# Loading V by head group, fewer zero blocks, and a load that waits for a ring buffer

## Chip, core and metric

The kernel runs on one core of one Trainium2 chip. The metric is the device time of one execution in microseconds (us), as the median of several runs. The core has a matrix engine (TensorE, PE in the profile, with its weight loads as PEld), a vector engine (VectorE, DVE), a scalar engine (ScalarE, ACT), a general engine (GpSimd, POOL), a queue engine (SyncE, SP) and 16 DMA engines that move data between the main memory and the on-chip memory.

## What is computed

Softmax attention over 8 batches with 12 heads of 448 tokens and 64 elements, followed by a two-layer network with a SiLU between the layers:

```python
scores = scale * np.matmul(q, k.transpose(0, 1, 3, 2))      # q, k, v: (8, 12, 448, 64)
attn = softmax(scores)
x = np.matmul(attn, v)                                      # then (3584, 768), heads side by side
h = x @ w_in                                                # (768, 2048)
out = (h * 1 / (1 + np.exp(-h))) @ w_out                    # (2048, 768), float32
```

## The kernel before

The 12 heads of a batch are worked in three head groups of four heads. A unit `n` is one head group of one batch: units 0, 1 and 2 are the first batch's, units 3, 4 and 5 the second's, and so on. For each unit the kernel loads the raw keys (`load_k`, line 330) and the raw queries (`load_q`, line 338), each 224 KB as stored on the chip, and VectorE turns them by transposes (`turn_k`, lines 407 and 412, writes the tile `KT`; `turn_q`, line 424, turns the tile `rq` in place). TensorE makes scores `s` from both (`score`, line 460), ScalarE takes their exponentials (lines 505 and 516, tiles `T` and `E`), and TensorE multiplies these with columns of ones for the sums and with V for the result `a` (`attend_alone`, line 568, for the first units; lines 582 and 615 later). VectorE transposes and inverts the sums (lines 640, 648 and 655, tile `rdn`) and scales `a` into `xT` (`norm`, line 685, or 674 for half units). The two products of the network run at line 697, as filler between the attention of later units in the beginning and alone in the end.

All loads go out on POOL's queue in one order, written out by hand near line 1215: keys and queries of unit 0 (its queries in two parts), of unit 1, then the keys of unit 2, the first batch's V in four loads, the queries of unit 2, the keys and queries of unit 3, six loads of `w_in`, and so on. V of a batch is a tile of 128 rows in which a load `x` (0 to 3) fills 32 rows; loads 0 and 1 of the first batch bring four tokens for each row and head, loads 2 and 3 three. In the first batch one load brings this for all twelve heads (192 KB or 144 KB); in later batches each head group has four loads of its own (64 or 48 KB). A rearrangement for unit 1 (`lift_v`, line 372) copies rows of V on VectorE once loads 0 and 1 are there, between the transposition and the inversion of unit 0's sums.

POOL has at most eight loads in flight: each load waits for the landing of the one eight places before it. Tiles come from rings of buffers: raw keys have two (`NRK`), raw queries four, V two. A load into a ring waits until the former tile of its buffer has been read. The raw keys of unit 2 are a special case in this kernel (`GUEST`): they go into a tile `room` that is carved from V's second buffer, which holds nothing until the second batch.

The order of all instructions on every engine is made when the program is built. A planner (class `Order`) runs a small clock with a cost for each operation, keeps a list of those that are ready, and writes the instructions down in the order of its clock; the chip then follows that order, and waits by semaphores. Before the first scores, and where the planner finds TensorE without work in the opening, it fills in products of zeros (`run_zeros`, line 2329), counted in blocks of 128 columns. `FIRST` is the number of blocks in the first such stretch.

```python
    COLD, FIRST, QUIET = 8.5, 47, 0.16
    ...
            if at is not None and len(self.sent) >= LOADS:
                at = max(at, self.sent[-LOADS].done + HOP)
```

Of the kernel before, what the change touches and what calls it, by code (L numbers as in the profile page):

```python
# [9 lines left out]
FP16 = mybir.dt.float16  # L10
# [204 lines left out]
def kernel(  # L215
# [11 lines left out]
    B, NH, S, D = q.shape  # L227
# [3 lines left out]
    NG = NH // HG  # L231
    TPP = S // 32
    NCH = 4
# [6 lines left out]
    NT = 2 * S // 128  # L240
    OH = DM // 2
    NRK, NRQ = 2, 4
    GUEST = (0, 2)
    PACE = 2.6
    BF0 = 4
    NPL = 4
    EAGER = 1
    HALVES = 0
    NEAR, LATE = 0.15, -0.3
    COLD, FIRST, QUIET = 8.5, 47, 0.16  # L250
    SHY = 0.5
    AWAIT = 1.0
    FAR = (NT * B // 4 - 1,)
# [27 lines left out]
    sb = ctx.enter_context(tc.tile_pool(name="sb", bufs=1))  # L281
# [40 lines left out]
    def group_of(src, b, hg):  # L322
        return src[b, HG * hg : HG * (hg + 1)].rearrange("h (i g) d -> (h i) (g d)", g=TPP)

    def load_k(b, hg):
        if (b, hg) == GUEST:
            t = guest
        else:
            t = sb.tile([128, TPP * D], FP16, name=f"rk_{b}_{hg}", tag="rk", bufs=NRK)
        nc.gpsimd.dma_start(out=t, in_=group_of(k, b, hg))  # L330
        rawk[(b, hg)] = t

# [7 lines left out]
    def form(b, hg):  # L340
        return "low" if b == 0 else ("low", "high")[(NG * b + hg) % 2]


    room = sb.tile([128, NH, NCH, D], FP16, name="room", tag="V", bufs=2)
    guest = room.rearrange("p h c d -> p (h c d)")[:, 0 : TPP * D]

    def first_v():
        VT[0] = sb.tile([128, NH, NCH, D], FP16, name="V_0", tag="V", bufs=2)
# [2 lines left out]
    def load_v(b, hg0, hg1, x):  # L351
        if b not in VT:
            VT[b] = sb.tile([128, NH, NCH, D], FP16, name=f"V_{b}", tag="V", bufs=2)
        hs = slice(HG * hg0, HG * hg1)
        kind = form(b, hg0)
        if x == 0 and b > 0 and NG * b + hg0 < ALONE:
            lo = 64 if kind == "low" else 0
            nc.gpsimd.memset(VT[b][lo : lo + 64, hs, place(b, hg0, NCH - 1), :], 0.0)
        first, count = X_TOK[kind][x]
        at = int(kind == "high" and count < NCH)  # L360
        nc.gpsimd.dma_start(  # L361
            out=VT[b][32 * x : 32 * (x + 1), hs, at : at + count, :],
            in_=v[b, hs].rearrange("h (i g) d -> i h g d", g=TPP)[
                :, :, first : first + count, :
            ],
        )
# [25 lines left out]
    def turn_k(b, hg, c0=0, c1=NCH):  # L392
        t = rawk[(b, hg)][:].bitcast(FP32).rearrange("p (g i) -> p g i", i=32)
        if c0 == 0:
            kt = sb.tile([128, TPP, 32, 2], FP16, name=f"KT_{b}_{hg}", tag="KT", bufs=3)
            KT[(b, hg)] = kt
        kt = KT[(b, hg)]
        pairs = kt.rearrange("p g i e -> p (g i e)").bitcast(FP32)
        pairs = pairs.rearrange("p (g i) -> p g i", g=TPP)
        high = form(b, hg) == "high"  # L400
        full = pairs[:, 2 * high : 2 * high + 12].rearrange("p (c x) i -> p x c i", x=4)
        for x in (0, 2):
            first, count = X_TOK[form(b, hg)][x]
            toks = t[:, first : first + 2 * count].rearrange("p (x c) i -> p x c i", c=count)
            at = int(high and count == 4)
            c2 = min(c1, NCH - 1)
            nc.vector.transpose(
                out=full[:, x : x + 2, c0:c2], in_=toks[:, :, at + c0 : at + c2]
            )
            if count == 4 and c1 == NCH:  # L410
                lone = 12 * (not high)
                nc.vector.transpose(out=pairs[:, lone : lone + 2], in_=toks[:, :, 3 - 3 * at])

    def turn_q(n, g0, g1):
        t = rawq[n][:].bitcast(FP32).rearrange("p (g i) -> p g i", i=32)[:, g0:g1]
        if units[n][0] == B - 1:

            to = sb.tile([128, TPP * D], FP16, name=f"q_{n}", tag="rq", bufs=NRQ)
            nc.vector.transpose(
                out=to[:].bitcast(FP32).rearrange("p (i g) -> p g i", g=TPP), in_=t  # L420
            )
            rawq[n] = to
        else:
            nc.vector.transpose(out=t, in_=t)  # L424
        QT[n] = rawq[n].rearrange("p (q e) -> p e q", e=2)
# [29 lines left out]
    def place(b, hg, c):  # L455
        return (c + 1) % NCH if form(b, hg) == "high" else c
# [714 lines left out]
    od = Order(SHY)  # L1171
    s_ring, m_ring, e_ring = Ring(3), Banks((0, 1)), Banks(range(NE))
    rk_ring, rq_ring, v_ring = Ring(NRK), Ring(NRQ), Ring(2)
    kt_ring, t_ring = Ring(3), Ring(NT_)
    ld_k, ld_q, ld_v, ld_win, ld_wout, wout_rows = {}, {}, {}, {}, [], []
    kt_op, qt_op, exp_op, rdn_op, x_op, g_op = {}, {}, {}, {}, {}, {}

    def plan_k(b, hg):
        ring = None if (b, hg) == GUEST else rk_ring
        ld_k[(b, hg)] = od.load(128, 2 * D * TPP, lambda: load_k(b, hg), ring)  # L1180

    def plan_q(n):
        ld_q[n] = [
# [6 lines left out]
            for g0, g1 in (PIECES if n == 0 else ((0, TPP),))  # L1190
        ]

    def plan_v(b, hg0, hg1):
        made = []
        for x in range(4):
            ring = v_ring if (x == 0 and hg0 == 0) else None
            heads, toks = HG * (hg1 - hg0), X_TOK[form(b, hg0)][x][1]
            made.append(
                od.load(32 * heads, 2 * D * toks, lambda x=x: load_v(b, hg0, hg1, x), ring)
            )  # L1200
        for hg in range(hg0, hg1):
            ld_v[(b, hg)] = made
# [9 lines left out]
    def plan_w_out(f0, f1):  # L1212
        wout_rows.append(f0)
        ld_wout.append(od.load(128 * (f1 - f0), 2 * DM, lambda: load_w_out(f0, f1)))

    plan_k(0, 0)
    plan_q(0)
    plan_k(0, 1)
    plan_q(1)
    plan_k(0, 2)  # L1220
    plan_v(0, 0, NG)
    plan_q(2)
    plan_k(1, 0)
# [7 lines left out]
    plan_q(5)  # L1231
    plan_w_out(0, 4)
    plan_v(1, 0, 1)
    plan_w_out(4, 8)
    plan_w_out(8, 12)
    plan_v(1, 1, 2)
    plan_w_out(12, 16)
    plan_v(1, 2, 3)
    for n in range(NB0 + NG, NU):
        b, hg = units[n][:2]  # L1240
# [6 lines left out]
    def plan_turns(upto):  # L1247

        while turned["n"] < min(upto, NU):
            if not plan_turn(turned["n"]):  # L1250
                return
            turned["n"] += 1

    def plan_turn(n):
        b, hg, g0, g1 = units[n]
        if b == B - 1 and not rq_ring.can(1, od.now):
            return False
        if (b, hg) not in kt_op:
            if not kt_ring.can(1, od.now):
                return False  # L1260
            kt_ring.take()
            first = Op(
                "DVE", 0.73, lambda: turn_k(b, hg), [ld_k[(b, hg)]], 20,
                then=None if (b, hg) == GUEST else rk_ring.give,
            )
            if n == 0:
                first = Op("DVE", 0.4, lambda: turn_k(b, hg, 0, 2), [ld_k[(b, hg)]], 20)
            kt_op[(b, hg)] = od.add(first)
        if b == B - 1:
            rq_ring.take()  # L1270
        qt_op[n] = [
            od.add(
                Op(
                    "DVE",
                    0.13 + (g1 - g0) / 30.0,
                    lambda g0=g0, g1=g1: turn_q(n, g0, g1),
                    [load],
                    20,
                    then=rq_ring.give if b == B - 1 else None,
                )  # L1280
            )
            for load, (g0, g1) in zip(ld_q[n], PIECES if n == 0 else ((0, TPP),))
        ]
        if n == 0:
            rest_k.append(
                od.add(
                    Op(
                        "DVE",
                        0.45,
                        lambda: turn_k(b, hg, 2, NCH),  # L1290
                        [kt_op[(b, hg)], qt_op[0][0]],
                        20,
                        then=rk_ring.give,
                    )
                )
            )
        return True
# [1129 lines left out]
```

## Time and profile before

| what | value |
|---|---|
| median of 3 runs | 377.55 us (377.43 to 378.58) |
| the profiled execution's own time | 377.82 us |
| its span, first to last instruction | 376.0 us |
| PE busy | 370.4 us, 98% of the span |
| DVE busy | 292.4 us, 78% |
| ACT busy | 255.6 us, 68% |
| POOL busy | 85.0 us, 23% |
| loads of the first 45 us, POOL's queue | 8.29 MB |
| DMA rate from 5 to 7 us, and from 13 to 15 us | 122 and 209 GB/s |

How to read it: lines such as `L361` are lines of the kernel. The page has the busy time by engine and by 40 slices of the span, and the chain of work that ended last, followed back from the end: what share of it lay on which engine. A timeline line gives the start in us, the time that it took, engine, line, operation, the tile written and read, and how many instructions are merged; in square brackets stands how long the engine was idle before it and what released it. A line of DMA issues gives the tiles, the queue, how many were issued, the size of one, and the time from its issue to its landing in us. A landing time of a single load below is its issue plus that time.

### The profile page before, as it was taken

To read this page: it belongs to the slowest core of one execution; us is meant where nothing else is said; L and a number is where in the kernel's file an instruction comes from. 1 tells how busy PE (TensorE), PEld (TensorE's weight loads), DVE (VectorE), ACT (ScalarE), POOL (GpSimd) and SP (SyncE) were. 2 spreads that over 40 slices of the span, in tenths; PEclk is the share of its full clock that TensorE was granted. 3 is DMA by queue.
4 is the path that set the end of the run, shared out by engine and by line. 5 is a ranking of instruction groups with operands and counts; after the bars stand their busy time and mean duration, and the time that the engine had idled before them with its cause. 6 is when DMAs were issued, how large, how long until landed. Compare 5 with 4: busy or idle time off the path is not lost.

```text
span 376.0 us, 10031 instructions
## 1 busy us (share of the span) xinstructions
PE 370.4 (98%) x4052; PEld 189.3 (50%) x4052; DVE 292.4 (78%) x613; ACT 255.6 (68%) x402; POOL 85.0 (23%) x155
## 2 busy tenths in 40 slices
PE   8999999999999999999999999999999999999996
PEld 3365445444444444444444444545556765556774
DVE  3667958999995969995969998899579744648883
ACT  4988873887878788777878777658872238883121
POOL 7552437424016326006423200000000000000000
PEclk9999999999999999999999999999999999999999
DMA  7999999919049948147964421210001241000144
GB/s 112 198 208 210 206 204 183 199 18 135 14 99 137 171 51 120 30 94 106 171 97 57 60 53 45 53 34 0 0 3 46 63 107 39 0 3 26 50 115 150
DMA packets 35967, 34.49 MB, mean 92 GB/s; under 512 B 11856, under 2 KB 35152, under 8 KB 35920
## 3 DMA queue, kind: packets, MB, share of 16 engines
q0 software_dynamic: 25312, 22.82, 41.1%
q1 hardware_dynamic: 10064, 10.40, 10.2%
q8 instruction: 32, 0.52, 0.6%
q10 hardware_dynamic: 544, 0.62, 0.5%
q14 instruction: 15, 0.12, 0.1%
HBM read 45.61 MB, written 11.01 MB: 151 GB/s over the span
## 4 chain that ended last, share of the span: by engine, by line
PE 97%; DMA 1%; issue 0%; POOL 0%; DVE 0%; POOLq 0%
PE p L697 28%; PE h L697 21%; PE f L697 16%; PE s L460 12%; PE a L582 8%; PE o L697 3%; PE a L568 2%; PE n_Q L697 2%; PE a L615 2%; PE n_P L697 2%; DMA rq<-in_q_dram 1%; PE z L2329 1%; PE z L697 0%; PE z L568 0%; DVE ost L1033 0%
## 5 line engine op out<-in xcount | busy, mean ns | idle before, releaser
L516 ACT ACTIVATE E<-s 128x896 f16<-128x896 f32 x164 | 142.0, 919 | 24.8 <-PE s L460 24.7
L697 PE MATMUL h<-xT,w_in_t 128*32 128x448 f16 (+2 forms) x762 | 83.5, 348 | 0.0
L697 PEld LDWEIGHTS <-w_in_t 128*128 128x128 f16 (+1 forms) x909 | 54.6, 97 | 50.0 <-issue 8.1
L361 POOL DMA_DIRECT2D V<-in_v_dram x88 | 48.5, 565 | 49.7 <-PE a L582 29.2
L697 PEld LDWEIGHTS <-G 128*128 128x128 f16 (+1 forms) x652 | 40.1, 97 | 26.0 <-issue 5.0
L729 ACT ACTIVATE th<-h 128x448 f16<-128x448 f32 x67 | 36.6, 546 | 24.3 <-PE h L697 20.7
L697 PE MATMUL p<-w_out_t,G 128*128 128x384 f16 (+1 forms) x294 | 46.7, 327 | 0.0
L460 PE MATMUL s<-rq,KT 32*128 32x448 f16 (+3 forms) x728 | 44.9, 347 | 0.5 <-DVE rq L424 0.5
L697 PEld LDWEIGHTS <-S 128*128 128x128 f16 (+1 forms) x329 | 29.9, 98 | 21.3 <-issue 3.4
L773 DVE SCALAR_TENSOR_TENSOR G<-th,h 128x448 f16<-128x448 f16 (+1 forms) x64 | 35.7, 573 | 4.7 <-ACT th L729 4.3
L697 PE MATMUL p<-D,S 128*128 128x384 f16 (+1 forms) x217 | 39.3, 327 | 0.0
L1027 ACT COPY ost<-p 128x384 f32<-128x384 f32 x36 | 17.3, 480 | 26.8 <-PE p L697 24.2
L582 PE MATMUL a<-E,V 128*32 128x448 f16 (+1 forms) x640 | 32.7, 356 | 0.0
L685 DVE SCALAR_TENSOR_TENSOR xT<-a,rdn 128x448 f16<-128x448 f32 x46 | 26.9, 618 | 3.4 <-PE a L582 2.2
L338 POOL DMA_DIRECT2D rq<-in_q_dram x25 | 13.9, 558 | 67.0 <-PE s L460 58.2
L460 PEld LDWEIGHTS <-KT 32*128 32x128 f16 (+1 forms) x824 | 12.4, 96 | 31.0 <-issue 29.2
L529 DVE TENSOR_TENSOR T<-T,E 128x1792 f16<-128x1792 f16 x21 | 22.8, 1086 | 4.8 <-ACT E L516 4.8
L529 DVE TENSOR_TENSOR T<-E,E 128x1792 f16<-128x1792 f16 x21 | 22.7, 1082 | 4.1 <-ACT E L516 4.0
L901 DVE TENSOR_TENSOR p<-f,p 128x448 f32<-128x448 f32 x15 | 9.3, 623 | 20.3 <-PE f L697 13.9
L1049 DVE TENSOR_TENSOR ost<-p,ost 128x384 f32<-128x384 f32 x28 | 15.4, 552 | 12.2 <-ACT ost L1027 7.7
L697 PE MATMUL f<-sx,tw 128*128 128x448 f16 x102 | 23.7, 353 | 0.0
L582 PEld LDWEIGHTS <-V 128*32 128x32 f16 (+1 forms) x640 | 13.5, 95 | 18.0 <-issue 10.1
(140 smaller groups left out, 483.9 us busy)
## 6 DMA issues: line engine op xcount, KB each, us to landing
out_dram<-ost SPq DMA_DIRECT2D x146, 48.0 KB, 2.2
rk<-in_k_dram POOLq DMA_DIRECT2D x23, 224.0 KB, 5.3
rq<-in_q_dram POOLq DMA_DIRECT2D x23, 224.0 KB, 5.9
w_out_t<-in_moe_w_out_dram POOLq DMA_DIRECT2D x4, 768.0 KB, 12.6
V<-in_v_dram POOLq DMA_DIRECT2D x42, 64.0 KB, 4.4
out_dram<-wide SPq DMA_DIRECT2D x48, 48.0 KB, 1.6
V<-in_v_dram POOLq DMA_DIRECT2D x42, 48.0 KB, 4.6
w_in_t<-in_moe_w_in_dram POOLq DMA_DIRECT2D x6, 256.0 KB, 9.2
```

Source lines behind the costliest of these rows:

```text
L338: nc.gpsimd.dma_start(out=rawq[n][:, cols], in_=group_of(q, b, hg)[:, cols])
L361: nc.gpsimd.dma_start(out=VT[b][32 * x : 32 * (x + 1), hs, at : at + count, :], in_=v[b, hs].rearrange("h (i g) d -> i h g d", g=TPP)[:, : ...
L460: nc.tensor.matmul(out=pS[p0 : p0 + 32 * (x1 - x0), h % 2, at : at + q1 - q0], lhsT=KT[(b, hg)][32 * h : 32 * (h + 1), key_rows(b, hg, c, ...
L516: nc.scalar.activation(out=E[(n, w)][:, 2 * y : 2 * y + 2, :], in_=pS_t[(n, w, y)][:, :, 0:S], func=AF.Exp, scale=attn_scale,)
L529: nc.vector.tensor_tensor(out=T[n], in0=T[n] if step else E[(n, 0)], in1=E[(n, step + 1)], op=ALU.add,)
L582: nc.tensor.matmul(out=a[32 * h : 32 * (h + 1), 0:S], lhsT=VT[b][k0:k1, HG * hg + h, place(b, hg, c), part - 1 :: 2], rhs=e[k0:k1, h], sta ...
L685: nc.vector.scalar_tensor_tensor(out=x3(b, cc)[:, cc % 3, 32 * g0 : 32 * g1], in0=acc[(n, part)][:, 0:nq], scalar=0.5, in1=rdn_t[n].rearra ...
L697: nc.tensor.matmul(out=out[i : i + cut], lhsT=w[:, i : i + cut], rhs=x, start=start, stop=stop, skip_group_check=True,)
L729: nc.scalar.activation(out=th, in_=h_t[(b, f, t0)][:, 0:n], func=AF.Tanh)
L773: nc.vector.scalar_tensor_tensor(out=dst[:, f, at + lo : at + hi], in0=th_t[(b, f, t0)][:, lo - t0 : hi - t0], scalar=1.0, in1=h_t[(b, f, ...
L1027: nc.scalar.copy(out=ost(qd, *OUT[m]), in_=bank(qd, BANK[m]))
L1049: nc.vector.tensor_tensor(out=t, in0=bank(qd, BANK[m]), in1=t, op=ALU.add)
```

## The change

Three things are changed. The first batch's V is loaded in eight loads: the four of the first head group (64, 64, 48 and 48 KB), then the four of the other two groups together (128, 128, 96 and 96 KB). The planner's own count stays at four loads; the last of them emits five. The first stretch of zeros has 44 blocks for 47, and the later stretches of the opening, which the planner sizes itself, come out as 9, 7, 9 and 13 blocks where they had 8, 11, 9 and 13. And the raw keys of unit 2 take a buffer of the ring of raw keys like all others, so their load waits until VectorE has turned the keys of unit 0; the tile `room` is gone. Apart from this every engine has the same instructions in the same order as before.

```diff
-    GUEST = (0, 2)
-    COLD, FIRST, QUIET = 8.5, 47, 0.16
+    COLD, FIRST, QUIET = 8.5, 44, 0.16
...
     def load_k(b, hg):
-        if (b, hg) == GUEST:
-            t = guest
-        else:
-            t = sb.tile([128, TPP * D], FP16, name=f"rk_{b}_{hg}", tag="rk", bufs=NRK)
+        t = sb.tile([128, TPP * D], FP16, name=f"rk_{b}_{hg}", tag="rk", bufs=NRK)
...
-    room = sb.tile([128, NH, NCH, D], FP16, name="room", tag="V", bufs=2)
-    guest = room.rearrange("p h c d -> p (h c d)")[:, 0 : TPP * D]
...
     def plan_k(b, hg):
-        ring = None if (b, hg) == GUEST else rk_ring
-        ld_k[(b, hg)] = od.load(128, 2 * D * TPP, lambda: load_k(b, hg), ring)
+        ld_k[(b, hg)] = od.load(128, 2 * D * TPP, lambda: load_k(b, hg), rk_ring)
...
+    def in_turn(b, hg0, hg1, x):
+        if b:
+            return load_v(b, hg0, hg1, x)
+        load_v(0, 0, 1, x)
+        if x == 3:
+            for y in range(4):
+                load_v(0, 1, NG, y)
+
     def plan_v(b, hg0, hg1):
...
-                od.load(32 * heads, 2 * D * toks, lambda x=x: load_v(b, hg0, hg1, x), ring)
+                od.load(32 * heads, 2 * D * toks, lambda x=x: in_turn(b, hg0, hg1, x), ring)
...
-                then=None if (b, hg) == GUEST else rk_ring.give,
+                then=rk_ring.give
```

More of the change, by code (lines that the diff above doesn't have):

```diff
@@ L1262, in plan_turn @@
             first = Op(
-                "DVE", 0.73, lambda: turn_k(b, hg), [ld_k[(b, hg)]], 20,
-                then=None if (b, hg) == GUEST else rk_ring.give,
+                "DVE", 0.73, lambda: turn_k(b, hg), [ld_k[(b, hg)]], 20, then=rk_ring.give
             )
```

## The prediction

> **What bounds the kernel now.** I read the page's head and its chain of waits first, then the chain for the first 45 us, then POOL's and DVE's timelines there, then single DMA issues with their time to landing. Of the page:
>
> ```profile
> span 376.0 us, 10031 instructions
> DMA  7999999919049948147964421210001241000144
> PE 97%; DMA 1%; issue 0%; POOL 0%; DVE 0%; POOLq 0%
> ```
>
> TensorE sets the end (97% of the chain). From 24 us on it never pauses, so what the opening loses or wins reaches the end one for one, and the change touches only the opening. There the DMA engines are full (the row of nines). The chain of waits from 0 to 45 us:
>
> ```profile
> 2.48 4.71 DMA rq<-in_q_dram
> ...
> 13.93 0.75 PE s L460 x8
> 14.68 0.57 issue
> 15.25 0.94 PE a L568 x16
> ...
> 19.90 0.65 PE s L460 x24
> 20.55 0.87 PE a L568 x16
> ```
>
> The 0.57 us before 15.25 are a wait for the first batch's V (the weights of that first `a` are V). After it TensorE runs on. What POOL issues meanwhile, and DVE's part where groups 2 and 3 arrive:
>
> ```profile
> 4.04 0.58 POOL L330 DMA_DIRECT2D room<-in_k_dram  x1
> 4.55 2.52 POOL L361 DMA_DIRECT2D V<-in_v_dram  x4
> 7.47 0.57 POOL L338 DMA_DIRECT2D rq<-in_q_dram  x1 [0.40 <-DMA rq<-in_q_dram]
> 9.40 0.55 POOL L330 DMA_DIRECT2D rk<-in_k_dram  x1 [1.36 <-DVE KT L412]
> 10.22 0.53 POOL L338 DMA_DIRECT2D rq<-in_q_dram  x1 [0.28 <-DMA rq<-in_q_dram]
> ...
> 6.01 0.20 DVE L407 STREAM_TRANSPOSE KT<-rk 128x64 f32<-128x64 f32 x1
> 18.89 0.65 DVE L424 STREAM_TRANSPOSE rq<-rq 128x448 f32<-128x448 f32 x1
> 19.46 0.61 DVE L640 STREAM_TRANSPOSE rdn<-a 128x448 f32<-128x448 f32 x1
> ```
>
> POOL starts each load only when the one eight places earlier has landed: its ninth and later loads follow a landing by 0.3 us (0.55 with a second wait). DVE turns the fourth q (group 0 of batch 1) at 18.89, as soon as it has landed.
>
> ```profile
> rq<-in_q_dram POOLq DMA_DIRECT2D x1, 224.0 KB, 8.3
> ...
> rk<-in_k_dram POOLq DMA_DIRECT2D x1, 224.0 KB, 8.8
> ...
> rq<-in_q_dram POOLq DMA_DIRECT2D x1, 224.0 KB, 8.6
> ...
> rq<-in_q_dram POOLq DMA_DIRECT2D x1, 224.0 KB, 4.0
> ```
>
> These are issues at 7.47, 9.40, 10.22 and 102.87 us: the first three stand 8 to 9 us in a full queue; the last one, alone, needs 4.0.
>
> **The change part by part.** The profiled execution took 377.82 us (span 376.0, 1.8 around it); the median of the runs is 377.55, so differences are worked out in the trace and added to 377.55.
>
> *Zero blocks, 47 to 44.* The first stretch (12 products, 1.00 to 6.04, 0.107 us a block) ends 0.32 earlier. The first score needs q turned at 5.42+0.41=5.83, and starts 0.05 after such a turn (7.62 to 7.67), so at 5.88 for 6.04: at most 0.16 won. Later stretches lose three more blocks in sum (9, 7, 9, 13 for 8, 11, 9, 13) under ACT's cover: ACT runs from 6.66 to 16.48 without a pause. ACT's third exponential needs the second score (7.67 to 8.25), which doesn't move, so no more than 0.1 passes on. I take 0, bounds -0.16 and, should the clock rise late, +0.9 (below).
>
> *V of head group 0 first.* Its four loads (64, 64, 48, 48 KB) need not wait for all 672 KB. Keys of group 2 landed at 4.04+7.6=11.7, and the 192 KB V loads behind it landed at 4.55+7.9=12.4 and 1.0 later, so 224 KB more are there by 12.9, well before 14.68. The 0.57 us wait goes. How much is kept: the next score's second half writes a bank that ACT frees at 15.68 and now starts at 16.13, so at most 0.45; with the zero blocks at most 0.55 in all. DVE's copy of V rows (14.66, before the reciprocal) now waits for the first two of the second four loads; issued near 9.2 and 9.8 they land by about 13.9 with the stream: covered by 0.7. The last V load is needed at 18.97 only.
>
> *Group 2's raw keys in the buffer of group 0's.* The load now waits until DVE has turned group 0's keys (6.01+0.20). POOL starts it at about 6.5 instead of 4.04. Queued behind it on POOL stand all eight V loads, then q2, k and q of batch 1, all w_in; SP's queue isn't touched. The landing itself hardly moves: q1, ahead of it in the stream, lands only at 9.95, and one load behind it is 11.1 to 11.7. Its scores come at 17.50, 5 us after its turn.
>
> *Eight loads for four.* POOL spends 4 x 0.54 = 2.2 us more (the pace of V loads at 42.5 to 44.1). Worse, the eight loads in flight now hold fewer bytes (all of V's 672 KB takes eight places, not four). With the eight-back rule: 6.5 (keys), V at 7.05, 7.6, 8.1, 8.7, 9.2, 9.8, 10.4; the last V load must wait for the keys' landing, 11.66+0.28, so 11.9; q2 at 12.5, k(1,0) 13.1, q3 13.6, where it was 7.47, 9.40, 10.22. By then the stream has almost run dry: the last V load lands near 11.9+2.3=14.2 (2.3 is a lone 64 KB load at 111.60). So q2 pays the lone latency: 12.5+4.0=16.5 (15.8 before). The next two follow at 1.25 us (two neighbours at 113.76 and 114.31 landed 3.9 and 4.6 after issue, so 1.25 apart): 17.75 and 19.0. In the window of 10 to 20 us one 16 KB instruction fetch occupies one engine for 0.96 us (0.6% of 16 engines in 10 us); before, k(1,0) landed 2.4 after q2, so I read it as hitting this pair, and add it: q3 at 19.96, before 10.22+8.6=18.85. It is 1.1 us later.
>
> *Who waits for that.* DVE turns q3 at 18.89, then `rdn` at 19.46, which frees the bank of the `a` at 20.48 (0.41 spare); further down the same row of DVE work, `xT` at 21.13 to 22.29 lets `a` start at 22.47, with 0.2 spare, the least. So TensorE is 1.1-0.2=0.9 us later, and what V won at 15 us is waited away at 20. Later loads shift by the same 1.1 or less, and TensorE by then stands 0.9 later itself.
>
> Bounds of that term: with no idle queue and no fetch on the path, q3 lands as before and TensorE keeps up to -0.45; with 4.6 for the lone load (issue at 181.03), 1.25 twice and a fetch that costs all of k's excess (2.4-1.15=1.25), q3 is at 20.85, +2.0, so +1.8. I take 0.9: the spacing rows are two neighbours with the same sizes. Sum: 0 - 0.57 + 0.57 (waited again) + 0.9 = +0.9, so 377.55+0.9=**378.45 us**; the profiled execution would be 378.7.
>
> By the Trainium skill, *DMA: Bandwidth & Descriptors*, "Rules for kernel authors", transfers of 64 KB and less are mostly overhead and should be joined. Rows here: V loads issued at 42.50 (64 KB) and 43.04 land 9.2 and 8.9 us later, so 0.24 us apart, which bytes alone explain. By the rule with a fixed 2 us for each of the four added loads in series, an estimate from that page, the time would be some 8 us more, 385.5; the rows deny it while the queue is full, and it gets no chance.
>
> **The rivals.**
> *A, not slower:* the stream never runs dry. For it: keys 1 and q1 land late (8.8, 9.95) and V's bytes go on behind them, so q2 may still find a queue, and loads behind a queue land 1.1 apart. It decides at a landing of q3 of 19.05, 0.2 late: with it on time -0.2 is left of V's gain, 0.25 sooner -0.45; about 377.2. Against it: q2's issue moves by 5 us.
> *B, more than that:* early loads land faster because POOL writes no descriptors from 4.1 to 6.5 (the DMA rate is only 122 GB/s from 5 to 7 us, 205 later). Even then ACT's unbroken row caps the gain at 0.55: 377.0.
> *C, dry sooner:* the keys, issued at 6.5, land as slowly as keys 1 did (issued 3.00, landed 8.83: 5.8 us), at 12.3. The last V load and all behind it start 0.65 later, q3 1.75 late: 377.55+1.55=379.1.
> *D, the clock:* the pause before the first score (5.71 to 5.88) keeps the clock low longer. A block took 0.107 us up to 6.04 and 0.064 in the stretch at 8.25, so the rise came about 6. Staying low to 9 would double the scores at 6.04 (+0.5) and 8.89 (+0.9), and ACT would be up to 0.9 late: partly under the late q3, so 378.9. The Trainium skill, *TensorE: Matmul & The Clock Gate*, Part 1, has the clock judged over free-running windows of 3.4 us; by that rule a 0.17 us pause in one is nothing, and an unlucky phase hits both kernels alike. No row tells which.
>
> **How the numbers follow.** Forecast (q3 0.5 to 1.9 late): 0.58; A 0.16; B 0.05; C 0.14; D 0.07. 0.3% is 1.13 us, about what a measurement here can tell from no change: below 376.42 or above 378.68. The forecast's own range, 377.85 to 379.4, lies half beyond 378.68 as the fetch falls (0.29); with C and half of D that makes slower 0.46; the other half of the forecast, A, half of D and the rest make same 0.50; faster gets 0.04 out of B's share, for a cap that I misread, since nothing found reaches -1.13. Range 377.0 to 379.9: from B's cap to C with a fetch's excess (+0.8) on top.
>
> **What would show it.** In the profile after: no idle time before the first `a` with V, near 14.7; POOL's keys of group 2 near 6.5, q2 near 12.5, q3 near 13.6; DVE's turn of q3 near 20 with idle time before it that names the DMA; TensorE idle near 20 to 21 us; all of it unchanged from 45 us on but for the shift. Wrong if q3's turn stays at 18.9 (A), if the keys land after 12 (C), or if the zero blocks at 8 us still take 0.107 each (D).

## The result, and the profile after

| | before | after |
|---|---|---|
| median, runs of the same session | 377.47 us (377.23 to 378.58, 8 runs) | 379.23 us (378.71 to 381.08, 8 runs) |
| ratio after to before | | 1.0053, 95% interval 1.0038 to 1.0069 |
| the profiled execution's own time | 377.82 us | 379.20 us |
| its span | 376.0 us | 377.3 us |

The changed kernel is 0.53% slower, 1.8 us by the medians, and more than the 0.3% that can be told from no change. The two profiled executions stand 1.38 us apart, since the one of before lies 0.35 above its median.

The head of the page after, and its chain of work that ended last:

```profile
span 377.3 us, 10038 instructions
...
PE 88%; DMA 8%; POOL 1%; DVE 1%; issue 1%; POOLq 0%
```

TensorE held 97% of this chain before. Now 88% of it is left, and DMA has 8%: loads have come onto the path. The chain from 0 to 45 us shows which ones (start, duration, what):

```profile
6.51 4.48 DMA rk<-in_k_dram
...
11.28 0.49 POOL V L354
...
16.26 10.26 DMA w_in_t<-in_moe_w_in_dram
...
27.07 13.57 DMA rq<-in_q_dram
...
40.66 0.65 DVE rq L417
...
41.86 1.30 PE h L690 x6
```

These lines go from the load of unit 2's keys through the last V load, which waits for those keys' landing, and through a `w_in` load to the queries of unit 5, which land at 27.07 + 13.57 = 40.6 us. VectorE turns them, and a product of the network starts late behind it. POOL in the opening:

```profile
6.51 0.53 POOL L326 DMA_DIRECT2D rk<-in_k_dram  x1 [2.44 <-DVE KT L400]
7.03 3.92 POOL L354 DMA_DIRECT2D V<-in_v_dram  x7
11.28 0.58 POOL L354 DMA_DIRECT2D V<-in_v_dram  x1 [0.32 <-DMA rk<-in_k_dram]
11.85 0.57 POOL L334 DMA_DIRECT2D rq<-in_q_dram  x1
```

POOL stands idle for 2.44 us before the keys. Then it issues without a pause until 17 us, but for the 0.32 before the last V load. The queries of unit 2 (`q2`) start at 11.85; before it was 7.47. What TensorE and VectorE make of it, with the first scores of unit 2 before the change as the line ahead:

```profile
17.50 0.77 PE L460 MATMUL s<-rq,KT 32*128 32x224 f16 x16
```

```profile
14.45 0.56 PE L561 MATMUL a<-T,V 128*32 128x448 f16 x8
...
18.59 0.58 PE L453 MATMUL s<-rq,KT 32*128 32x224 f16 x16 [1.59 <-DVE rq L417]
...
41.86 1.30 PE L690 MATMUL h<-xT,w_in_t 128*128 128x448 f16 x6 [0.30 <-DVE G L766]
```

```profile
17.89 0.65 DVE L417 STREAM_TRANSPOSE rq<-rq 128x448 f32<-128x448 f32 x1 [1.31 <-DMA rq<-in_q_dram]
20.01 0.65 DVE L417 STREAM_TRANSPOSE rq<-rq 128x448 f32<-128x448 f32 x1 [0.29 <-DMA rq<-in_q_dram]
```

The first product with V starts at 14.45 and no longer waits (15.25 before). That lead of 0.8 is lost at 18.59, where TensorE waits 1.59 us for `q2` (this score stood at 17.50 before), and from 19 us on each product starts 0.9 later than before. At 41.86 this becomes 1.37 (the same product stood at 40.49), and it stays so.

One reason why `q2` is late is the DMA rate. Below are three stretches of 2 us, before and then after. The columns are: busy time and number of instructions on PE, PEld, DVE, ACT and POOL, granted clock, mean load of the DMA engines, GB/s.

```profile
11.00:13.00 2.00, 2.00 (x31) 0.55 (x19) 0.76 (x3) 2.00 (x3) 1.00 (x2) 1.00 1.51 192
13.00:15.00 2.00, 1.68 (x26) 0.53 (x24) 0.96 (x3) 2.00 (x4) 1.62 (x3) 1.00 1.32 209
15.00:17.00 2.00, 1.75 (x32) 0.74 (x36) 1.59 (x5) 1.75 (x3) 1.59 (x3) 1.00 1.13 207
```

```profile
11.00:13.00 2.00, 2.00 (x28) 0.64 (x20) 0.76 (x3) 2.00 (x4) 1.72 (x4) 1.00 1.15 135
13.00:15.00 2.00, 2.00 (x36) 0.76 (x32) 0.95 (x3) 2.00 (x4) 2.00 (x4) 1.00 1.18 152
15.00:17.00 2.00, 2.00 (x35) 0.54 (x24) 1.47 (x4) 2.00 (x4) 1.95 (x3) 1.00 1.13 151
```

The stream of loads runs at 135 to 152 GB/s where it ran at 192 to 209. At 11.0 us before had 1,568 KB issued and not landed (keys of unit 2, all of V, `q2`, keys and queries of unit 3). After, where the keys had just landed, had 576 KB: seven V loads, none of them over 128 KB. By 13.0 us it is 1,120 KB against 1,664 KB.

A second reason is likely: one late part. A load ends in 16 parts. Of `q2`'s, fifteen were there by 16.89 us and the last at 17.87. A 16 KB instruction fetch stood on a DMA engine from 15.42 to 17.15 us (1.73 us); before, it stood there from 16.07 to 16.96, when `q2` had landed. The trace does not say which engine carried the late part, so that the fetch made up about 1 us of the 2.15 by which `q2` landed late is not shown.

### The profile page after: what moved, and what is told of

Read it like the earlier page. It is cut to its first block, busy times and chain, and to the rows that moved or that the text cites. A ratio compares the mean times of both kernels' runs of the same rounds, so it can differ in the third digit from the quotient of the medians.

```text
span 377.3 us, 10038 instructions
## 1 busy us (share of the span) xinstructions
PE 370.3 (98%) x4051; PEld 189.2 (50%) x4051; DVE 292.2 (77%) x613; ACT 255.6 (68%) x402; POOL 87.0 (23%) x159
## 4 chain that ended last, share of the span: by engine, by line
PE 88%; DMA 8%; POOL 1%; DVE 1%; issue 1%; POOLq 0%
PE p L690 28%; PE h L690 18%; PE f L690 16%; PE s L453 9%; PE a L575 8%; DMA rq<-in_q_dram 5%; PE o L690 3%; DMA w_in_t<-in_moe_w_in_dram 3%; PE n_Q L690 2%; PE a L608 2%; PE n_P L690 2%; DMA rk<-in_k_dram 1%; POOL w_in_t L372 1%; PE a L561 0%; POOL rk L326 0%
## 5 line engine op out<-in xcount | busy, mean ns | idle before, releaser
L354 POOL DMA_DIRECT2D V<-in_v_dram x92 | 50.5, 562 | 51.2 <-PE a L575 29.2
L690 PEld LDWEIGHTS <-S 128*128 128x128 f16 (+1 forms) x329 | 29.9, 98 | 21.2 <-issue 3.4
L453 PEld LDWEIGHTS <-KT 32*128 32x128 f16 (+1 forms) x824 | 12.5, 96 | 33.0 <-issue 29.8
L894 DVE TENSOR_TENSOR p<-f,p 128x448 f32<-128x448 f32 x15 | 9.4, 624 | 20.3 <-PE f L690 13.9
```

Source lines behind the costliest of these rows:

```text
L354: nc.gpsimd.dma_start(out=VT[b][32 * x : 32 * (x + 1), hs, at : at + count, :], in_=v[b, hs].rearrange("h (i g) d -> i h g d", g=TPP)[:, : ...
L453: nc.tensor.matmul(out=pS[p0 : p0 + 32 * (x1 - x0), h % 2, at : at + q1 - q0], lhsT=KT[(b, hg)][32 * h : 32 * (h + 1), key_rows(b, hg, c, ...
L690: nc.tensor.matmul(out=out[i : i + cut], lhsT=w[:, i : i + cut], rhs=x, start=start, stop=stop, skip_group_check=True,)
```

## The experiments

Three names are used below. Theory N: the number of loads is the cost (places in the window of eight, and POOL's 0.55 us for each). Theory P is N at work after a stall: POOL, once late, issues without a pause, and small loads feed the stream too slowly. Theory G: the wait of unit 2's keys is the cost. Ratios are to runs of before on the same chip, with 95% intervals; 0.1% is 0.38 us.

**V in eight loads, alone.** The edit, to the kernel before:

```diff
+    def in_turn(b, hg0, hg1, x):
+        if b:
+            return load_v(b, hg0, hg1, x)
+        load_v(0, 0, 1, x)
+        if x == 3:
+            for y in range(4):
+                load_v(0, 1, NG, y)
```

> The kernel before with the first batch's V in eight loads and nothing else: the third group's keys still go into V's idle buffer, 47 zero blocks. Theory N (number of loads): a load starts only when the one eight places earlier has landed, so with eight small V loads in the eight places q2, k and q of batch 1 start near 12.0 to 13.6 us for 7.5 to 10.2, the stream of loads thins out and q2 lands 1 to 2 us late: +0.9 to +1.8 us against before, most of the change's whole +1.76. Theory G (the keys' wait is what starves the stream, POOL idle from 4.1 to 6.5): without that wait V's first group arrives early and nothing is late: -0.5 to 0.

Measured: 378.53 us for 377.62, ratio 1.0035 (1.0018 to 1.0052). N's time holds, and G falls as the only cause: with the keys' load at 4.03 us and POOL never kept waiting for a buffer, the loss is there. POOL waited 0.4 to 0.9 us before each of the last four V loads for the landing eight places back, and `q2` started at 11.47. By itself this is about two thirds of the change's loss.

N's way to that time does not hold. `q2` landed at 15.47, 0.25 sooner than before, where 1 to 2 us late was expected, and up to 56 us TensorE stands 0.2 ahead of the trace of before. But the `w_in` loads behind are 0.9 late at their median part, and the lag stays. TensorE falls behind at the first product with `w_out` (0.1 at 56.7 us) and at 73 to 76 us (0.5), behind queries that landed at 70.13 for 68.85. POOL's timeline, and VectorE's at those queries:

```profile
8.73 0.58 POOL L361 DMA_DIRECT2D V<-in_v_dram  x1 [0.92 <-DMA rk<-in_k_dram]
...
11.47 0.57 POOL L338 DMA_DIRECT2D rq<-in_q_dram  x1
```

```profile
70.15 0.65 DVE L424 STREAM_TRANSPOSE rq<-rq 128x448 f32<-128x448 f32 x1 [0.47 <-DMA rq<-in_q_dram]
```

**The keys' wait, alone.** The edit, to the kernel before:

```diff
-    GUEST = (0, 2)
...
-        if (b, hg) == GUEST:
-            t = guest
...
-        ring = None if (b, hg) == GUEST else rk_ring
```

> The kernel before with one part of the change: the third group's keys wait for a buffer of raw keys; V in four loads, 47 zero blocks. Theory N: POOL's loads start at 6.5 (keys), 7.1 to 8.9 (V), 9.5 (q2), 10.1 (k), 10.7 (q3), which the full stream still hides: -0.1 to +0.3 us. Theory G: the stream has 224 KB less in flight from 4.6 to 7 us and never gets it back, loads land 1 us or more late: +1.0 to +1.8.

Measured: 377.93 for 377.62, ratio 1.0009 (1.0001 to 1.0018): 0.3 us, at the upper edge of N's range and far below G's. The keys started at 6.59, `q2` at 9.55 and landed 0.36 later than before; from the first `w_in` load to unit 5's queries, landings agree with before within 0.25 us (the median parts are 0.6 to 0.8 late). Here the stall of 2.5 us on POOL, with large loads behind it, is nearly made good.

**44 zero blocks, alone.**

```diff
-    COLD, FIRST, QUIET = 8.5, 47, 0.16
+    COLD, FIRST, QUIET = 8.5, 44, 0.16
```

> The kernel before with 44 zero blocks for 47 and nothing else. Theory: the first score starts 0.15 us earlier (5.9 for 6.04), of which ACT's row passes on 0 to 0.1: -0.15 to +0.05 us. Rival D (the pause before the first score keeps the clock low): +0.5 to +1.0, and the blocks at 8 us take 0.107 each.

Measured: 377.47 for 377.62, ratio 0.9999 (0.9990 to 1.0008). Rival D is out. In the trace the first score came at 6.02, not 5.9, since its queries landed 0.13 later; the pause before it was there.

**V in six loads, keys in the idle buffer, 44 zero blocks.**

```diff
+    SPLIT = (2, 3)
+        if b or x not in SPLIT:
+            return load_v(b, hg0, hg1, x)
+        load_v(0, 0, 1, x)
+        if x == 3:
+            for y in SPLIT:
+                load_v(0, 1, NG, y)
```

> The kernel before with 44 zero blocks and V in six loads: x 0 and x 1 whole, then x 2 and x 3 of head group 0, then x 2 and x 3 of the other two groups; the keys still go into V's idle buffer. Head group 0's V is then complete 192 KB earlier in the stream, some 0.9 us at the 205 GB/s of before. Theory N: the loads behind start at 9 to 12 us, while some 600 KB or more are still queued, so nothing of the stream is lost and the wait of 0.57 before the first product with V goes: -0.55 to -0.3 us. Rival (each added small load costs the stream its own fixed time, some 0.4 us): -0.1 to +0.5, with q2 landing 0.5 to 1 us late.

Measured: 378.24 for 377.62, ratio 1.0011 (1.0001 to 1.0022); the theory's gain is missed. The rival's time came, though `q2` landed 0.4 sooner than before and not later. In the one trace the wait at 15 us is gone, TensorE stands 0.33 ahead of the trace of before, and no `w_in` load lands later. But this execution took 377.48, the fastest of eleven. What the slower ones lost was not traced.

**The changed kernel with the idle buffer given back.** The edit, to the changed kernel:

```diff
+    GUEST = (0, 2)
...
+        ring = None if (b, hg) == GUEST else rk_ring
```

> The changed kernel with one part undone: the third group's keys go into V's idle buffer again; V in eight loads and 44 zero blocks stay. If the parts simply add (V in eight alone measured +0.35%, the keys' wait alone +0.09%, the zero blocks 0), this is +0.8 to +0.9 us against before, and the changed kernel's other 0.9 us come only from both parts together. Theory P (POOL's pace: after its stall from 4.1 to 6.5 it issues without a pause to 13.5, and small loads of 64 and 48 KB every 0.55 us supply less than the stream can carry) says the same, +0.5 to +1.0, with the w_in loads about 0.9 us late instead of 2.5. Rival (the loss is all in the eight loads, and the difference of the first runs is scatter): +1.6 to +1.9.

Measured: 378.92 for 377.66, ratio 1.0031 (1.0019 to 1.0043). So eight loads with the idle buffer lose about 1.2 us, and without it 2.0. The 1.2 lies between P's range (up to 1.0) and the rival's (from 1.6). The wait that costs 0.3 alone costs 0.8 on top of eight loads; that difference between intervals is likely, not certain. The expected 0.9 us for the `w_in` loads held at the first of them and had grown to 1.7 by the sixth. (Such lags of the stream are those of the median of a load's 16 parts; a landing is the last part.)

**V's first four loads ahead of the keys.** The edit, to the changed kernel; the second four stay behind the keys:

```diff
-        load_v(0, 0, 1, x)
-        if x == 3:
-            for y in range(4):
-                load_v(0, 1, NG, y)
+        load_v(0, 1, NG, x)
...
+    def after_v(b, hg):
+        if (b, hg) == (0, 2):
+            for x in range(4):
+                load_v(0, 0, 1, x)
+        load_k(b, hg)
```

> The changed kernel with one place in POOL's queue changed: the four loads of V's first head group go ahead of the third group's keys, so POOL has work from 4.1 to 6.5 us while the keys' buffer is still in use; eight V loads, no idle buffer used, 44 zero blocks. Theory P: POOL's stall is filled, keys start at 6.5 as in the changed kernel, q2 near 11, and the stream is about 0.9 us late at the w_in loads (as with the eight loads alone) for 2.5: +0.3 to +1.0 us against before. Rival G (the keys themselves come too late): they land later still, behind 224 KB of V, near 11.5 to 12, so no better than the changed kernel: +1.6 to +2.0.

Measured: 378.78 for 377.66, ratio 1.0034 (1.0021 to 1.0047): 1.1 to 1.3 us, between P's range and G's and nearer to P's. The keys landed 0.2 later than before and 0.8 later than in the changed kernel, at no cost (at 17.5 us TensorE is 0.5 ahead of before), and the first `w_in` load was 0.7 late for 2.45. The stall was worth about 0.7 us of the loss; the eight loads kept the rest.

**`q2` ahead of the last two V loads.**

```diff
         if x == 3:
-            for y in range(4):
-                load_v(0, 1, NG, y)
+            load_v(0, 1, NG, 0)
+            load_v(0, 1, NG, 1)
+
+    def then_v(n, g0, g1):
+        load_q(n, g0, g1)
+        if n == 2:
+            load_v(0, 1, NG, 2)
+            load_v(0, 1, NG, 3)
```

> The changed kernel with q2 taken ahead of the last two of V's eight loads, nothing else. POOL's stall and the number of loads are those of the changed kernel. Theory P: q2 starts near 10.4 for 11.85 and brings 224 KB into a queue that only held small loads, so it lands near 15.5 to 16.5 for 17.87, the wait of 1.6 us at 17 goes and the w_in loads are 1.5 to 2.2 us late for 2.5: +0.4 to +1.2 us against before. Rival (the stream's rate, not POOL's order, is low while POOL writes descriptors): what q2 gains k and q3 lose, and the w_in loads stay 2.5 late: +1.3 to +2.0.

Measured: 379.40 for 377.66, ratio 1.0053 (1.0039 to 1.0067): nothing won. The rival's time came, and what `q2` gained unit 3's queries lost, as it said. `q2` landed at 16.22 as expected, and the wait only moved on. TensorE's timeline of this kernel:

```profile
17.72 0.58 PE L453 MATMUL s<-rq,KT 32*128 32x224 f16 x16 [0.51 <-DVE rq L417]
...
21.05 0.40 PE L453 MATMUL s<-rq,KT 32*64 32x224 f16 x15 [0.60 <-DVE rq L417]
```

Less is lost at 17.7, and what is saved there is lost again at 21.05, at unit 3's queries, which landed 1.46 late. The `w_in` loads were 1.8 to 2.0 late, within P's bounds and not the rival's 2.5; P's price for that lag was too low.

**V in five loads, keys in the idle buffer, 44 zero blocks.** The edit, to the kernel of six:

```diff
-    SPLIT = (2, 3)
+    SPLIT = (3,)
```

> The kernel before with 44 zero blocks and V in five loads: x 0 to 2 whole, x 3 of head group 0, then x 3 of the other two groups; the keys still go into V's idle buffer. Head group 0's V is then complete 96 KB earlier in the stream, 0.47 us at 205 GB/s. If one added load costs the stream nothing: -0.4 to -0.1 us. If each added load costs what six loads seem to (their median +0.1% in spite of the wait removed): 0 to +0.3.

Measured: 377.63 for 377.66, ratio 0.9999 (0.9991 to 1.0008). One added load costs nothing; the wait at 15 us that it removes brings nothing in the median either.

**Unit 5's keys and queries ahead of three `w_in` loads**, in the changed kernel and, as its control, in the kernel before.

```diff
-    plan_w_in(1024, 2048)
     plan_k(1, 2)
     plan_q(5)
+    plan_w_in(1024, 2048)
```

> The changed kernel with the loads of keys and queries of unit 5 taken ahead of the three w_in loads of 512 KB (they come 7.5 us of stream earlier, those w_in loads 2.2 us later). In the changed kernel's trace unit 5's queries land at 40.63, 2.2 late, and hold DVE and then TensorE at 41.86 (offset +0.91 before, +1.37 behind). Theory S (the lag of the stream of loads lands on TensorE twice, at q2 and at these queries): the wait at 41.86 goes and the offset stays +0.9: +0.8 to +1.4 us against before, 0.4 to 0.9 less than the changed kernel. Rival (the first wait, at q2, sets all, or the lag only finds the next load): +1.6 to +2.1.

> The same move of unit 5's keys and queries on the kernel before: the control for the run before this one. No wait for these queries stands in the trace of before (they land at 38.45 and are turned at once), and the three w_in loads come 2.2 us later but before their first product: -0.3 to +0.3 us against before by theory S and by its rival. More than +0.3 would say that the move itself costs, and has to be taken off the other run.

Measured: 379.99 for 377.60, ratio 1.0067 (1.0053 to 1.0082), and for the control 377.75, ratio 0.9998 (0.9989 to 1.0007). The changed kernel with the move lost 2.5 us, more than either range. Theory S, that the lag bites at `q2` and at these queries and nowhere else, falls. TensorE's timeline in the changed kernel with the move:

```profile
41.81 0.55 PE L690 MATMUL h<-xT,w_in_t 128*128 128x448 f16 x2 [1.42 <-DMA w_in_t<-in_moe_w_in_dram]
```

The same place is now held by a `w_in` load, and for longer (in this execution, the slowest of its six, the stream was over 3 us late, and `q2` had landed 2.8 late before the move could matter). The move itself is free where the stream is on time.

**V in five loads, four of them ahead of the keys; no idle buffer** (the aims of the change with larger loads).

```diff
+        if (b, hg) == (0, 2):
+            for x in range(3):
+                load_v(0, 0, NG, x)
+            load_v(0, 0, 1, 3)
+        load_k(b, hg)
```

> The changed kernel's aims with other loads: V in five loads (x 0 to 2 whole, x 3 of head group 0, x 3 of the rest), the first four of them ahead of the third group's keys, which wait for a buffer of raw keys; no idle buffer used, 44 zero blocks. POOL then has large loads to start from 4.1 to 6.5 us and the window of eight holds as many bytes as before. Theory P and S: w_in loads within 0.3 us of before, V in time for the first product: -0.3 to +0.3 us against before, 1.5 less than the changed kernel. Rival (the keys' wait costs by itself, since they land near 13.5 and their turn holds DVE ahead of the first normalisation at 14): +0.5 to +1.0.

Measured: 378.00 for 377.60, ratio 1.0014 (1.0003 to 1.0024). The 0.4 to 0.5 us lie between P's range and the low end of the rival's. P is right about the stream: no `w_in` load lands later than before, and of the changed kernel's 2.0 us about 1.5 are gone. The rival's mechanism is there too. VectorE's timeline:

```profile
13.80 0.38 DVE L400 STREAM_TRANSPOSE KT<-rk 128x192 f32<-128x192 f32 x1 [3.71 <-DMA rk<-in_k_dram]
```

The keys, now behind 576 KB of V, are turned at 13.80 for 11.68 and push the first normalisation from 13.98 to 14.49.

**Four loads of 256 bytes behind V's four** (read by nobody).

```diff
+    aside = const.tile([32, 4, 4], FP16, name="aside")
...
+        if b == 0 and x == 3:
+            for y in range(4):
+                nc.gpsimd.dma_start(out=aside[:, y, :], in_=v[0, 0][32 * y : 32 * (y + 1), 0:4])
```

> The kernel before with four added loads of 256 bytes each (32 partitions x 4 numbers, never read) behind V's four loads; V, keys' buffer and the 47 zero blocks as before. It moves no bytes to speak of, only takes four places of the eight and four of POOL's 0.55 us. Theory N (places and POOL's time are the cost of the eight loads): q2, k and q of batch 1 start near 12.0 to 12.7, 13.0 to 13.8 and 13.8 to 14.5 us for 7.5, 9.4 and 10.2, loads from w_in on are 0.5 to 1.5 us late, and the time is +0.5 to +1.5 us against before, about that of V in eight loads alone (+1.3 by its ratio). Rival (V's cut rows, 64 and 48 KB over 32 partitions, move more slowly by themselves): with V uncut nothing is lost, -0.1 to +0.3.

Measured: 379.19 for 377.57, ratio 1.0046 (1.0032 to 1.0060). The loss, 1.6 to 1.7 us, is just above N's range, and so is the lag of the `w_in` loads (2.0 to 2.4 at the median part). This decides for N against cut rows of V: V's loads, the keys' buffer and the zeros are those of before, 1 KB is added, and nearly the whole loss of the change is there. Nor is it the added bytes' own transfer: their 128 packets took 2.9 us in sum, 0.2 us of 16 engines. POOL's timeline, and two stretches of 2 us (columns as above):

```profile
6.98 0.59 POOL L1198 DMA_DIRECT2D aside<-in_v_dram  x1
8.30 0.51 POOL L1198 DMA_DIRECT2D aside<-in_v_dram  x1 [0.73 <-DMA rk<-in_k_dram]
9.45 0.49 POOL L1198 DMA_DIRECT2D aside<-in_v_dram  x1 [0.65 <-DMA rq<-in_q_dram]
10.63 0.49 POOL L1198 DMA_DIRECT2D aside<-in_v_dram  x1 [0.69 <-DMA room<-in_k_dram]
11.70 0.58 POOL L339 DMA_DIRECT2D rq<-in_q_dram  x1 [0.58 <-DMA V<-in_v_dram]
```

```profile
13.00:15.00 2.00, 2.00 (x36) 0.76 (x32) 1.08 (x3) 2.00 (x4) 1.93 (x4) 1.00 1.07 135
15.00:17.00 2.00, 2.00 (x36) 0.55 (x24) 1.89 (x5) 2.00 (x4) 2.00 (x4) 1.00 0.95 127
```

Three of the small loads and then `q2` each wait 0.58 to 0.73 us for the landing eight places back; the small ones bring nothing, and `q2` starts at 11.70 for 7.47. From 13 us, as V ends (13.85), the stream falls to 135 and 127 GB/s. `q2` still lands only 0.33 later than before, and at 17.5 us TensorE is 0.3 ahead; it is 0.5 behind at 26 us, 1.2 at 41, 1.6 at 57 and 2.7 at 76. (This execution took 380.31, 1.1 above the median of its runs.)

By the Trainium skill, *DMA: Bandwidth & Descriptors*, "Rules for kernel authors", transfers under 64 KB are mostly overhead and should be joined. The direction agrees with this run; the size is 1.6 us for four loads, not the 8 that a fixed 2 us for each in series would give, an estimate from that page.

**The lag of the stream and the time.** The landing of the first `w_out` load (42.22 us before) is a measure of the stream behind the opening. From the traces (issue plus time to landing), with the time of the same execution:

| kernel | landing against before, us | profiled execution, us | ratio of the runs |
|---|---|---|---|
| before | 0 | 377.82 | 1 |
| five V loads | -0.19 | 377.33 | 0.9999 |
| six V loads | -0.12 | 377.48 | 1.0011 |
| keys' wait alone | +0.07 | 377.66 | 1.0009 |
| eight V loads alone | +0.75 | 378.42 | 1.0035 |
| eight, idle buffer, 44 | +1.11 | 378.36 | 1.0031 |
| V first, then keys | +1.25 | 378.32 | 1.0034 |
| `q2` in the middle | +1.89 | 379.12 | 1.0053 |
| the change | +1.94 | 379.20 | 1.0053 |
| four loads of 256 bytes | +2.22 | 380.31 | 1.0046 |
| the change, unit 5 moved | +3.54 | 381.26 | 1.0067 |

Where TensorE loses its time is not the same place each time: in the changed kernel at `q2` and at 41.9 us, in the kernel of eight V loads alone not before 56 us, with the 256-byte loads from 22 to 76 us. What these kernels share is that the stream is late and stays late. Lags up to 0.1 go with no loss against before's execution; 0.75 to 1.25 go with 0.5 to 0.6 us, 1.9 with 1.3 to 1.4, 2.2 and 3.5 with 2.5 and 3.4 (the last two executions lie 1.1 and 1.3 above the medians of their kernels). These are single executions, so this goes together and no more. The rows left out are the control (+0.36, 377.88), the zeros alone (-0.32, 378.27, where TensorE lost 0.6 us more than before at 127 us, which nothing here explains) and the last five-load kernel (-0.62, 377.85).

No version beat the kernel before: 44 zero blocks, five loads with the idle buffer, and the moved loads of unit 5 are as fast as it.

## Why the prediction was right or wrong

**Zero blocks, taken as 0:** right. The first score came at 5.89 (5.88 forecast), and alone the part measures 0.9999.

**V's first head group, wait of 0.57 gone and the gain waited away later:** right. The first product came 0.80 sooner (14.45), and the second half of the next score, where the cap of 0.55 stood, 0.56 sooner. One term was short: the second four loads' first two landed at 13.82 and 14.54, not by 13.9, and VectorE's copy waited 0.20 us for them, at no cost (14.67 for 14.66).

**The keys' load at 6.5, its landing hardly moved:** right, 6.51 and 11.00 (11.66 before). That the part alone costs little was implied and holds, at 0.3 us. What I did not see is that it costs more together with eight loads.

**Issues behind eight V loads:** right within 0.7. Forecast were 11.9, 12.5, 13.1 and 13.6 for the last V load, `q2`, keys and queries of unit 3; it was 11.28, 11.85, 12.40 and 12.93.

**"q2 pays the lone latency: 12.5+4.0=16.5":** wrong, and the first step that failed. I let V land by 14.2 and gave `q2` an empty queue. V's last load landed at 15.82 and `q2` at 17.87, 6.0 us after its issue. The stream had been at 135 to 152 GB/s since 11 us, and I priced it as an idle queue at one moment, and not as a lower rate over 6 us. Fifteen of `q2`'s parts were there at 16.89, near the 16.5; the last 0.98 came with an instruction fetch of 1.73 us, which I had put at 0.96 and on the two loads behind. The row for the 4.0, at 102.87, was not a lone load either: two output stores of 48 KB were issued 0.3 us before and 0.15 after it.

**"q3 at 19.96":** the number came true (19.98) by other terms than mine. The wait that I expected for it at 20 to 21 us stood at 17.0 to 18.6 for `q2` instead. Its net cost, 0.9, was the forecast's: luck, in number and in cost.

**"Later loads shift by the same 1.1 or less, and TensorE by then stands 0.9 later itself":** wrong, and the step that the size of the loss hung on. The loads behind were 2.3 to 2.5 us late at the median of their parts and 1.1 to 2.2 at landing, not 1.1 or less (1.1 held up to unit 4's queries at 29.9 us; from 33 us it was 1.7 to 2.2), and with TensorE 0.9 later the rest came out at 41.86 as another 0.46. So the sum is +1.37 in the traces where I had 0.9, and about +1.8 in the medians, to which the offset of 0.3 between before's profiled execution and its median adds. Two runs moved a load out of the way, `q2` and unit 5's queries, and the lag was lost at the next load each time.

**The rivals.** A and B are out: the stream did thin. C's condition, the keys landing after 12, was not met (11.00), though its time, 379.1, is the one nearest to the result; running the keys later still (11.83, with POOL's stall filled) was faster. D is out by the run of the zeros alone, and the granted clock is 1.00 in every 2 us from 1 to 23 us of both traces, also where a block took 0.107 us. The rule of the Trainium skill, given no chance at 8 us, pointed the right way.

The chances were 0.50 for no change and 0.46 for slower, and the range of 377.0 to 379.9 held the 379.23. The sign was right, and so was the cause in kind, a stream that thins behind eight small loads. The load that TensorE waits for was another, the size was half, and slower came, to which I had given the smaller chance. 379.23 lies at the top of the forecast's own range, which stood for a q3 of some 20.7; q3 came at 19.98, and the rest came from a later wait that I had put at nothing, so the fit of the range is partly luck.

**Open.** Whether a place in the window or POOL's 0.55 us is the limit depends on the kernel as far as the traces show: with the 256-byte loads POOL waits before nearly every load, in the changed kernel it issues without a pause. No run varied the one without the other. Why the stream moves only 135 to 152 GB/s with 0.6 to 1.1 MB issued and not landed is not settled either. The traces show one thing that goes with it. Packets of the loads that took over 0.4 us (at the median they take 0.15 us or less) number 2 between 8 and 20 us before, and 0 to 4 in the kernels of five and six V loads, of 44 zero blocks and of the control. They number 18 with eight V loads alone, and 30 each in the changed kernel and with the 256-byte loads, where they held the engines for 20 to 21 us in sum; the other kernels lie between, the keys' wait alone with 12. What holds them is not shown. That POOL is busy issuing is not enough: in the kernel of five V loads it was busy for 1.92 of the 2 us from 13 to 15, and the stream ran at 211 GB/s. There is one trace for each kernel, and which load decides in the other executions can differ.

## What to carry to other kernels

A queue that allows only so many loads in flight, as here, can be read as a budget of bytes: splitting a load, or adding one of 256 bytes, takes a place and issue time from the large loads behind it. Before splitting a load to get one part early, count the bytes in flight after the split against those before, and follow the lag of the whole stream to its next consumers, not only to the first: here it was paid up to some 60 us after it arose. A stall of the issuing engine was nearly made good where large loads followed it, and was kept where small ones did.

## What the runs showed of the hardware

Four added loads of 256 bytes in a full stream cost 1.6 us (0.46%), no less than cutting V's 672 KB into eight does alone (0.35%). From 11 to 17 us, with eight V loads of 48 to 128 KB in the queue and three of 224 KB issued behind them, the 16 DMA engines moved 135 to 152 GB/s; with V in loads of 144 and 192 KB they moved 192 to 209. And a lag of the stream that arose by 21 us was still there at 60 us: the keys and queries that landed at 58.4 and 59.6 before landed 1.8 later in the changed kernel.
